# Attention through packed queries, then a squared-ReLU layer pair: two loads of the second layer's weights one place earlier, any PSUM bank for two stages, and a new order of the work

## The chip, the cores and the metric

The kernel runs on one core of one Trainium2 chip. The metric is device time in microseconds (us) of one execution; the kernel before takes 233.85 us (median of 3 runs, 233.79 to 234.32). TensorE (PE) multiplies matrices, VectorE (DVE) and ScalarE (ACT) work element by element, GpSimd (POOL) here issues nearly all loads, and SyncE (SP) issues the stores and some transposing transfers. Products of TensorE land in PSUM, eight banks of 512 float32 values in each of 128 partitions.

## The reference

```
def sm_attn(qq, kk, vv):
    s = scale * np.matmul(qq, kk.transpose(0, 1, 3, 2))
    s = s - np.max(s, axis=-1, keepdims=True)
    a = np.exp(s)
    a = a / (np.sum(a, axis=-1, keepdims=True) + 1e-09)
    return np.matmul(a, vv)
p_packed = sm_attn(p, k, v)
out = sm_attn(q, p_packed, p_packed)
...
x = out.transpose(0, 2, 1, 3).reshape(B * S, H * D)
h = x @ w_in
r = np.maximum(h, 0.0)
return (r * r) @ w_out
```

There are 8 batches of 8 heads, 576 tokens, 64 columns a head, and 32 packed queries p a head. So x has 4608 rows of 512 columns; w_in is 512 x 2048 and w_out 2048 x 512. All inputs and the output are float32; the kernel computes in bfloat16 with float32 sums.

## The kernel before

The kernel works batch by batch, and the stages of several batches overlap. For a batch b it does this, in pieces that the code names by letters, the batch, and a part:

- Tk, Tq: k and q are transposed into kT and qT (L703, L700), on VectorE for batches 0 to 4 and by transposing transfers of SP for 5 to 7.
- S1: scores of the packed queries (L736), MX their maximum (L755), EX their exponential on ScalarE (L763), E its transposes on TensorE (L769), EC the copy of these to SBUF (L611 on VectorE, L609 on ScalarE), PV the product with v (L783).
- XN, XQ, XM, XC: the packed result is divided by its sum (L792), and transposed in two ways (L796, and L802 with the copy L611).
- M: the packed result times w_in, four pieces of 512 columns (L813), and MC, their casts to bfloat16. The first layer is thus applied to the 32 packed rows of each head, and the tokens follow by the second softmax.
- S2: scores of q against the packed result (L830); SI, SM, SU transpose them and take off the maximum (L851, L857, L861), SE is the exponential on ScalarE (L864), SS the sum and its reciprocal (L867, L868), SN the division (L874), SO the transpose back into a2 (L878). For batch 0 this goes in three parts of 128, 192 and 256 tokens (SO.0.0, SO.0.1, SO.0.2), for batch 1 in two of 256 and 320 (SO.1.0, SO.1.1).
- F (batches 0 and 1, L915) or F1 (the others, L887): the first layer's output, a2 with M; R the ReLU (L923 on ScalarE, L925 on VectorE, and L897), Q or SQ the square (L933 on ScalarE, L935 on VectorE, and L905, L907) into gT. F.0.1.2 is block 2 of part 1 of batch 0.
- F2: the second layer for 128 tokens, 16 matmuls that add up over w_out's 16 blocks (L941). F2.3.1 is block 1 of token tile 3. FC copies the sum out and ST stores it (L953). For most token tiles of batches 2 to 7 a scheme with seven products of halves takes its place (GS and WS, sums of gT and w_out on VectorE, L986; GP the products, L1008; GC the adding up, L1028).

Before a wait of TensorE that the plan foresees, `keep_clock` (L615) issues matmuls on zeros, called fills here, to hold TensorE's clock.

The order is not written by hand. Each piece is an entry with its engines, its needs, and the PSUM banks or buffers it takes; `Plan.forward` goes through time as its own durations have it, and of the pieces that could start takes the one of the lowest level plus a value from `TABLE`. The order that comes out is the order of the instructions on each engine. Some groups keep the order in which they were added: all loads are one line, set by the string `ORDER`, where k0 stands for the two loads of batch 0's k, v and q alike, x and y for batch 0's q in two parts, a0 to a3 for w_in (4 pieces each), b0 to b7 for w_out, two of its 16 blocks each. A load is issued when the load eight places before it has landed (`issued[-8]`). A matmul F2 of block fb needs `LWO.(fb // 2)`, the load b(fb // 2).

E and PV take one bank each from `ONES[:3]` (banks 4, 5, 6) for batches 0 and 1, and from `ONES` (4 to 7) later; F2's tiles of batch 0 take theirs from `ONES` too. S1, S2, M and F take pairs of the banks 0 to 5 (`PAIRS`). A bank comes free when the last piece that reads it has ended, such as MC for M.

Of the kernel before, what the change touches and what calls it, by code (L numbers as in the profile page):

```python
# [14 lines left out]
P = 128  # L15
# [26 lines left out]
class Plan:  # L42
# [177 lines left out]
ORDER = ("k0 v0 x0 a0 y0 a1 a2 a3 k1 b0 b1 v1 b2 q1 b3 b4 b5 b6 b7 "  # L220
# [7 lines left out]
TABLE = {'o': {'Lk.0.0i': -36.900503, 'Lk.0.1i': 0.41924, 'Lk.0.0': -16.56608, 'LP.0': 169.009326, 'Lk.0.1':  # L228
# [292 lines left out]
def kernel_impl(tc, q, k, v, p, w_in, w_out, out):  # L521
# [23 lines left out]
    with ExitStack() as ctx:  # L545
# [485 lines left out]
        add = plan.add  # L1031
        PAIRS = [(0, 1), (2, 3), (4, 5)]
        ONES = [(4,), (5,), (6,), (7,)]
        OUTS = [(6,), (7,)]
        RS = [(8 + i,) for i in range(NR)]
        OS = [(14 + i,) for i in range(NO)][::-1]
        OP = [(14 + i, 15 + i) for i in range(0, NO - 1, 2)]
# [362 lines left out]
```

## Time and profile before

| | |
|---|---|
| median of 3 runs | 233.85 us (233.79 to 234.32) |
| the profiled execution | 233.42 us, of which the span from the first to the last instruction is 231.7 us |
| PE busy in the span | 220.0 us, 95%; 13.9 us of these are fills |
| DVE busy | 199.4 us, 86% |
| ACT busy | 148.4 us, 64% |
| POOL busy | 60.5 us, 26% |
| granted clock of TensorE | 0.994 |
| read and written in HBM | 37.22 and 9.44 MB |

In rows of a timeline the first number is the start, the second the time from the first start to the last end of the merged instructions, then engine, line, operation, tiles and shapes, and the count; in brackets stands how long the engine was idle before, and what ended it. Instructions of one engine overlap a little at their ends, so the distance from one start to the next is shorter than a length.

### The profile page before, as it was taken

To read this page: it belongs to the slowest core of one execution; us is meant where nothing else is said; L and a number is where in the kernel's file an instruction comes from. 1 tells how busy PE (TensorE), PEld (TensorE's weight loads), DVE (VectorE), ACT (ScalarE), POOL (GpSimd) and SP (SyncE) were. 2 spreads that over 40 slices of the span, in tenths; PEclk is the share of its full clock that TensorE was granted. 3 is DMA by queue.
4 is the path that set the end of the run, shared out by engine and by line. 5 is a ranking of instruction groups with operands and counts; after the bars stand their busy time and mean duration, and the time that the engine had idled before them with its cause. 6 is when DMAs were issued, how large, how long until landed. Compare 5 with 4: busy or idle time off the path is not lost.

```text
span 231.7 us, 6374 instructions
## 1 busy us (share of the span) xinstructions
PE 220.0 (95%) x2613; PEld 160.0 (69%) x2630; DVE 199.4 (86%) x336; ACT 148.4 (64%) x243; POOL 60.5 (26%) x108
## 2 busy tenths in 40 slices
PE   8978899999999999999999999999999999999991
PEld 5655664456654476768777877787668888888880
DVE  3679978999989999999999899999999997958340
ACT  3324994268955899775997936859988988310100
POOL 9787646333243575640000000000000000000010
PEclk9999999999999999999999999999999999999997
DMA  7999999999999999999999659757041001515325
GB/s 235 188 161 180 184 204 205 203 193 251 241 229 223 223 219 195 158 148 126 177 193 166 135 94 207 149 83 172 0 96 43 4 0 35 113 36 114 70 52 174
DMA packets 46668, 34.06 MB, mean 147 GB/s; under 512 B 25376, under 2 KB 38368, under 8 KB 46640
## 3 DMA queue, kind: packets, MB, share of 16 engines
q0 software_dynamic: 19488, 18.09, 50.5%
q1 hardware_dynamic: 26304, 14.98, 31.4%
q10 hardware_dynamic: 848, 0.59, 0.9%
q8 instruction: 20, 0.33, 0.6%
q14 instruction: 8, 0.07, 0.1%
HBM read 37.22 MB, written 9.44 MB: 201 GB/s over the span
## 4 chain that ended last, share of the span: by engine, by line
PE 83%; DVE 6%; DMA 5%; POOL 1%; issue 1%; ACT 1%; DVEq 0%; ACTq 0%; POOLq 0%
PE ps L1008 32%; PE ps L887 21%; PE ps L941 15%; PE ps L915 4%; PE ps L813 3%; DMA v_b<-in_v_dram 3%; DMA kq_b<-in_q_dram 2%; PE ps L959 2%; DVE gT L935 1%; PE ps L783 1%; PE ps L830 1%; PE ps L736 1%; PE ps L769 1%; POOL v_b L624 1%; DVE qT L700 1%
## 5 line engine op out<-in xcount | busy, mean ns | idle before, releaser
L897 ACT ACTIVATE r_b<-ps 128x576 bf16<-128x576 f32 x86 | 50.4, 663 | 10.1 <-PE ps L887 9.7
L887 PE MATMUL ps<-a,M 128*128 128x288 bf16 x384 | 52.3, 286 | 0.2 <-issue 0.2
L887 PEld LDWEIGHTS <-M 128*128 128x128 bf16 x384 | 37.3, 98 | 11.1 <-issue 0.2
L941 PE MATMUL ps<-w_out_b,gT 128*128 128x512 bf16 x159 | 41.3, 380 | 1.1 <-issue 0.6
L1008 PEld LDWEIGHTS <-gT 128*128 128x128 bf16 x384 | 36.9, 98 | 7.3 <-issue 1.3
L609 ACT CAST M<-ps 128x1024 bf16<-128x1024 f32 (+1 forms) x30 | 26.9, 933 | 12.4 <-PE ps L813 12.3
L609 ACT COPY o_sb<-ps 128x512 f32<-128x512 f32 (+1 forms) x23 | 12.9, 568 | 32.2 <-PE ps L1008 18.4
L1008 PEld LDWEIGHTS <-gS 128*128 128x128 bf16 x288 | 27.8, 98 | 4.5 <-issue 0.7
L953 POOL DMA_DIRECT2D out_dram<-o_sb x3 | 1.7, 556 | 108.8 <-ACT o_sb L609 103.6
L1028 DVE TENSOR_TENSOR o_sb<-o_sb,ps 128x512 f32<-128x512 f32 x30 | 20.3, 676 | 10.1 <-PE ps L1008 10.0
L907 DVE TENSOR_TENSOR gT<-r_b 128x1152 bf16<-128x1152 bf16 x37 | 27.1, 746 | 1.6 <-ACT r_b L897 1.6
L941 PEld LDWEIGHTS <-gT 128*128 128x128 bf16 x176 | 16.2, 98 | 15.4 <-issue 2.1
L1008 PE MATMUL ps<-wS,gT 128*128 128x256 bf16 x192 | 24.0, 273 | 0.0
L1008 PE MATMUL ps<-w_out_b,gT 128*128 128x256 bf16 x192 | 23.5, 273 | 0.0
L1008 PE MATMUL ps<-wS,gS 128*128 128x256 bf16 x192 | 23.3, 273 | 0.0
L923 ACT ACTIVATE r_b<-ps 128x512 bf16<-128x512 f32 (+2 forms) x30 | 17.8, 659 | 4.8 <-PE ps L915 4.7
L915 PE MATMUL ps<-a,M 128*128 128x256 bf16 (+3 forms) x160 | 18.3, 262 | 2.2 <-DVE a L878 1.0
L915 PEld LDWEIGHTS <-M 128*128 128x128 bf16 x160 | 14.0, 97 | 6.8 <-issue 2.2
L763 ACT ACTIVATE e<-ps,n 128x576 bf16<-128x576 f32 x16 | 11.7, 737 | 7.8 <-DVE n L755 7.6
L615 PE MATMUL ps<-o_sb 128*128 128x256 bf16 x89 | 13.9, 319 | 1.1 <-DVE o_sb L618 1.1
L755 DVE TENSOR_REDUCE n<-ps 128x1 f32<-128x576 f32 x16 | 11.6, 748 | 3.1 <-PE ps L736 3.0
L864 ACT ACTIVATE e<-s 128x1152 bf16<-128x1152 f32 (+4 forms) x11 | 10.0, 912 | 6.2 <-DVE s L861 6.1
(77 smaller groups left out, 322.0 us busy)
## 6 DMA issues: line engine op xcount, KB each, us to landing
out_dram<-o_sb SPq DMA_DIRECT2D x65, 128.0 KB, 3.5
kq_b<-in_k_dram POOLq DMA_DIRECT2D x14, 288.0 KB, 11.1
kq_b<-in_q_dram POOLq DMA_DIRECT2D x10, 288.0 KB, 8.7
w_in_b<-in_moe_w_in_dram POOLq DMA_DIRECT2D x16, 128.0 KB, 5.7
w_out_b<-in_moe_w_out_dram POOLq DMA_DIRECT2D x8, 256.0 KB, 9.6
v_b<-in_v_dram POOLq DMA_DIRECT2D x5, 320.0 KB, 11.8
v_b<-in_v_dram POOLq DMA_DIRECT2D x12, 128.0 KB, 8.7
v_b<-in_v_dram POOLq DMA_DIRECT2D x5, 256.0 KB, 12.2
```

Source lines behind the costliest of these rows:

```text
L609: nc.scalar.copy(dst, src)
L615: nc.tensor.matmul(half(7)[:, :2 * P], lhsT=zero[:, :P], rhs=zero, start=True, stop=True)
L755: nc.vector.tensor_reduce(n1[b % 2][:, qd:qd + 1], ps1[b, qd], axis=AX.XY if b in XBAR else AX.X, op=ALU.max, negate=True)
L763: nc.scalar.activation(e_out(qd) if b in XBAR else e1[:, qd, :S], ps1[b, qd], ACT.Exp, bias=n1[b % 2][:, qd:qd + 1], accum_out=d1[b % 2][: ...
L887: nc.tensor.matmul(t[:, c], lhsT=M[b % 2][:, qd, fb * FB:(fb + 1) * FB], rhs=a2[b % 2][:, qd, c * HALF:(c + 1) * HALF], start=(qd == 0), s ...
L897: nc.scalar.activation(dst, src, ACT.Relu)
L907: eng.tensor_tensor(out=dst, in0=r, in1=r, op=ALU.mult)
L915: nc.tensor.matmul(t[:, c, m * w:(m + 1) * w], lhsT=M[b % 2][:, qd, fb * FB:(fb + 1) * FB], rhs=a2[b % 2][:, qd, o:o + w], start=(qd == 0) ...
L923: nc.scalar.activation(dst, ph["h", b, x, j], ACT.Relu)
L941: nc.tensor.matmul(po[t], lhsT=gT[:, fb, n0:n0 + P], rhs=w_out_b[:, fb, :], start=(fb == 0), stop=(fb == NFB - 1))
L1008: nc.tensor.matmul(pz[g, k][:, i], lhsT=a[:, f, i * P:(i + 1) * P], rhs=w[:, f], start=(k not in ON and h == 0 and f == 0 and i == 0), sto ...
L1028: nc.vector.tensor_tensor(out=oC(g, i, j), in0=oC(g, *src), in1=pz[g, z], op=ALU.add)
```

## The change

Two places move in the order of loads: b0 goes ahead of batch 1's k, and b3 ahead of batch 1's q. In the built program GpSimd's queue therefore issues w_out's first piece before k1's two loads, and its fourth before q1's three. All other loads keep their order.

E and PV of batches 0 and 1 may take any of the eight banks. In the built program batch 0's still stand in bank 4; batch 1's two E are in banks 0 and 1 and its PV in bank 0, where they were in 4, 5 and 5.

`TABLE` has new values throughout, so all engines have a new order. In the first 51 us the programs differ as follows: VectorE does SS.0.0 and SI.0.2 between SI.0.1 and SO.0.0, takes the casts MC.0.0.0 and MC.0.1.1 and the ReLU R.0.1.1 and three more, and leaves the cast MC.0.2.0, one ReLU, five of batch 0's twelve squares, EC.0.0, EC.1.0 and the two casts of M.1 that it had to ScalarE, while two squares come to it from there. TensorE has F.0.1.3, F.0.0.3 and six matmuls of F2 ahead of S1.1, where one of F2 stood, and F.0.2.5, F.0.2.6 behind it. There are 97 fills for 89. Every piece before F.1.0.0 in one program stands before it in the other. On SP the stores of 11 tiles stand ahead of batch 5's key transposes for 9.

```
-ORDER = ("k0 v0 x0 a0 y0 a1 a2 a3 k1 b0 b1 v1 b2 q1 b3 b4 b5 b6 b7 "
+ORDER = ("k0 v0 x0 a0 y0 a1 a2 a3 b0 k1 b1 v1 b2 b3 q1 b4 b5 b6 b7 "
           "k2 v2 q2 k3 v3 q3 k4 v4 q4 k5 v5 q5 k6 v6 q6 k7 v7 q7")
...
-TABLE = {'o': {'Lk.0.0i': -36.900503, 'Lk.0.1i': 0.41924, 'Lk.0.0': -16.56608, 'LP.0': 169.009326, 'Lk.0.1':
...
         ONES = [(4,), (5,), (6,), (7,)]
         OUTS = [(6,), (7,)]
+        ANY = ONES + [(i,) for i in range(4)]
...
                 add(f"E.{b}.{qd}", [("PE", 0.28, lambda u, b=b, qd=qd: s1_tr(b, qd, u))], [f"EX.{b}.{qd}"] + (["I"] if b == 0 else []),
-                    line="E", take=[ONES[:3] if b < 2 else ONES], level=L + 1)
+                    line="E", take=[ANY if b < 2 else ONES], level=L + 1)
...
-                line="PV", take=[ONES[:3] if b < 2 else ONES], mode=2, level=L + 1)
+                line="PV", take=[ANY if b < 2 else ONES], mode=2, level=L + 1)
```

More of the change, by code (lines that the diff above doesn't have):

```diff
@@ L226 @@
 XTURN = (5, 6, 7)
-TABLE = {'o': {'Lk.0.0i': -36.900503, 'Lk.0.1i': 0.41924, 'Lk.0.0': -16.56608, 'LP.0': 169.009326, 'Lk.0.1':
[290 rows of a table removed]
+TABLE = {'o': {'Lk.0.0i': -55.383072, 'Lk.0.1i': 25.361911, 'Lk.0.0': 69.070364, 'LP.0': 5.218882, 'Lk.0.1':
[291 rows of a table added]
 def kernel_impl(tc, q, k, v, p, w_in, w_out, out):
```

581 rows, old and new, of the table TABLE are left out of this document.

## The prediction

> **What bounds the kernel now.** I read the table of stretches first, then the chain that ended last, then the timelines of VectorE, TensorE, ScalarE and the GpSimd queue up to 64 us. Stretches: core, us, then busy time and count of PE, PEld, DVE, ACT and POOL, granted clock, DMA share, GB/s.
>
> ```profile
> 20.00:32.00 12.00, 10.16 (x136) 7.43 (x128) 11.40 (x27) 11.21 (x21) 7.91 (x14) 1.00 1.17 184
> 32.00:51.00 19.00, 18.48 (x222) 9.51 (x207) 16.29 (x32) 9.28 (x17) 8.60 (x14) 1.00 1.22 201
> 51.00:64.00 13.00, 12.80 (x99) 8.26 (x106) 12.53 (x27) 11.88 (x22) 4.32 (x8) 1.00 1.19 242
> 64.00:100.00 36.00, 35.22 (x563) 22.03 (x554) 34.84 (x57) 27.62 (x48) 20.53 (x38) 1.00 1.20 211
> 100.00:227.00 127.00, 126.42 (x1418) 101.05 (x1406) 112.03 (x164) 82.62 (x129) 3.24 (x6) 1.00 0.58 100
> ```
>
> The reader is to see that TensorE is the bound from 32 us on: from 64 to 227 us it is idle for 36 - 35.22 + 127 - 126.42 = 1.36 us. Its work is the same in both programs. So a new order can win or lose only what TensorE waits, or spends on matmuls that merely hold the clock (fills). Most of that lies before 32 us; from 20 to 32 us TensorE is idle 1.84 us, and VectorE is busy 11.40 of 12 us. One row gives the fills; the built programs have 89 before and 97 after.
>
> ```profile
> L615 PE MATMUL ps<-o_sb 128*128 128x256 bf16 x89 | 13.9, 319 | 1.1 <-DVE o_sb L618 1.1
> 17.68 1.27 PE L615 MATMUL ps<-o_sb 128*128 128x256 bf16 x10
> ```
>
> By the first row one lasts 0.32 on the mean, the slow ones at the very start among them; by the second ten take 1.27 us with the drain of the last, some 0.11 us each.
>
> **The change, step by step.** From the start to the first block of batch 1's first layer (F.1.0.0, 50.57 us) both programs do the same pieces, fills apart. The step is therefore to find F.1.0.0's new start; then the stretch to S1.2 (63.55 us); then the rest.
>
> *Batch 0's second softmax, on VectorE.* After q has landed (row 16.48) it is one unbroken chain.
>
> ```profile
> 16.48 0.65 DVE L700 STREAM_TRANSPOSE qT<-kq_b 128x448 f32<-128x448 f32 x1 [0.35 <-DMA kq_b<-in_q_dram]
> 17.05 0.38 DVE L867 TENSOR_REDUCE t<-e 128x8 f32<-128x256 bf16 x1
> 17.58 0.58 DVE L851 STREAM_TRANSPOSE s<-ps 128x384 f32<-128x384 f32 x1
> 18.91 0.30 DVE L878 STREAM_TRANSPOSE a<-n 128x128 f32<-128x128 f32 x1
> 19.14 0.67 DVE L851 STREAM_TRANSPOSE s<-ps 128x512 f32<-128x512 f32 x1
> 19.73 0.52 DVE L861 TENSOR_TENSOR s<-s,m 128x384 f32<-128x384 f32 x1
> 23.10 0.38 DVE L878 STREAM_TRANSPOSE a<-n 128x192 f32<-128x192 f32 x1
> 24.25 0.63 DVE L611 CAST M<-ps 128x512 bf16<-128x512 f32 x1
> 25.48 0.56 DVE L935 TENSOR_TENSOR gT<-r_b 128x768 bf16<-128x768 bf16 x1
> 26.25 0.45 DVE L878 STREAM_TRANSPOSE a<-n 128x256 f32<-128x256 f32 x1 [0.22 <-PE ps L915]
> 30.48 0.65 DVE L925 TENSOR_SCALAR r_b<-ps 128x512 bf16<-128x512 f32 x1
> ```
>
> I cost an instruction by the distance to the next start. SI.0.1 (17.58) can't start earlier, since it needs the scores of the q that landed last. In the new order SS.0.0 (17.05 to 17.58, 0.53) and SI.0.2 (19.14 to 19.73, 0.59) stand between SI.0.1 and SO.0.0, which were before SI.0.1 and after SO.0.0: SO.0.0 goes from 18.91 to 20.03. The cast MC.0.0.0 that comes to VectorE (0.55, row 24.25) and SM.0.0, SU.0.0 fit into its wait for q and cost nothing; so does EC.0.0, which ScalarE now does between its two exponentials: what is late from it ends in the same wait. SO.0.1: 4.19 before after SO.0.0, now without SI.0.2 and with MC.0.1.1 (0.55): 4.15, so 24.18 for 23.10. SO.0.2: 3.15 before, without the wait (0.22), the cast (0.55) and a square (25.48 to 26.03, 0.55), with R.0.1.1, a relu of 768 columns on VectorE. That form isn't in the trace: between 0.58 (row 30.48, 512 columns, to the next start) and 1.0 (the same by 768/512 and its length of 0.65); I take 0.85, as time grows with columns. It must await F.0.1.1, itself 1.1 late, so SO.0.2 comes at 27.0 for 26.25, +0.75. The eleven extra fills ahead of F.0.1.0 (97 against 86) lie in this wait, 11 x 0.11 = 1.2; they are no second charge.
>
> *TensorE up to S1.1.* Here the earlier w_out load pays.
>
> ```profile
> 26.89 1.08 PE L915 MATMUL ps<-a,M 128*128 128x256 bf16 x8 [0.29 <-ACT r_b L923]
> 28.26 1.91 PE L915 MATMUL ps<-a,M 128*128 128x256 bf16 x16 [0.28 <-DVE M L611]
> 30.69 0.60 PE L915 MATMUL ps<-a,M 128*128 128x256 bf16 x4 [0.19 <-ACT r_b L923]
> 31.43 0.70 PE L736 MATMUL ps<-kT,pT 32*32 32x512 bf16 x32
> 42.79 7.95 PE L941 MATMUL ps<-w_out_b,gT 128*128 128x512 bf16 x35
> ```
>
> F.0.2.0 moves from 26.89 to about 27.6. Then the waits of 0.28 and 0.19 and three fills (0.33) go, as six second-layer matmuls and F.0.1.3, F.0.0.3 stand there: 0.8 back. A second-layer matmul takes 7.95 / 35 = 0.22. S1.1 has 1.3 us more work ahead of it (six of those, 1.3, and 16 first-layer matmuls, 1.1, less F.0.2.5, F.0.2.6 and one second-layer matmul, 1.1): 31.43 + 0.75 - 0.8 + 1.3, about 32.7. This is order, not loss: TensorE stands level with the old program there.
>
> *The loads.* W_out piece 0 goes ahead of k1's two, piece 3 ahead of q1's three. GpSimd's queue, and the median times to landing of just these:
>
> ```profile
> 20.81 1.19 POOL L657 DMA_DIRECT2D kq_b<-in_k_dram  x2
> 22.09 1.41 POOL L694 DMA_DIRECT2D w_out_b<-in_moe_w_out_dram  x2
> kq_b<-in_k_dram POOLq DMA_DIRECT2D x2, 288.0 KB, 6.9
> w_out_b<-in_moe_w_out_dram POOLq DMA_DIRECT2D x2, 256.0 KB, 8.4
> kq_b<-in_q_dram POOLq DMA_DIRECT2D x2, 144.0 KB, 9.9
> q0 software_dynamic: 9774, 9.52, 98.3%
> ```
>
> The k1 pair lands around 28.0, the w_out pair around 30.8: 1.4 us a piece. So k1's second half comes at about 30.1 instead of 28.8, ahead of the transpose that VectorE reaches past 31 us; q1's last third comes at about 39.9 instead of 38.5. The issues cost GpSimd nothing new, since the queue (98.3% busy up to 60 us) is the limit. The Trainium skill says otherwise of such queues: on its page SBUF — State Buffer, in the box on the "DVE blocks DMA" trap, descriptors written by GpSimd starve while VectorE holds the port pair they share. By the rows above no starving is seen, the trace doesn't bear the rule out; by it the sum would be that of the last rival below.
>
> *Batch 1.*
>
> ```profile
> 37.81 0.22 PE L802 MATMUL ps<-ident,pp 128*128 128x128 bf16 x1
> 38.61 0.63 PE L813 MATMUL ps<-w_in_b,ppT 64*32 64x512 bf16 x16
> 39.09 1.01 ACT L609 CAST M<-ps 128x1024 bf16<-128x1024 f32 x1 [2.46 <-PE ps L813]
> 40.45 0.77 DVE L700 STREAM_TRANSPOSE qT<-kq_b 128x576 f32<-128x576 f32 x1
> 42.11 0.74 PE L830 MATMUL ps<-qT,pq 32*32 32x256 bf16 x32
> 42.68 1.45 DVE L851 STREAM_TRANSPOSE s<-ps 128x512 f32<-128x512 f32 x2 [0.35 <-PE ps L830]
> 49.96 0.44 DVE L878 STREAM_TRANSPOSE a<-n 128x256 f32<-128x256 f32 x1
> 50.57 2.43 PE L915 MATMUL ps<-a,M 128*128 128x256 bf16 x20
> ```
>
> The banks: batch 1's transposes and values move from 4 and 5 to 0 and 1, which S1.1 and the exponentials have given back by then; 4 and 5 open the last two of four second-layer tiles earlier. No instruction is added, cost nothing. From S1.1 to XM.1 it was 37.81 - 31.43 = 6.4 us: now 39.1. Seven second-layer matmuls (1.5) come before M.1.0: 40.7. Both of its first casts are now on ScalarE in a row; before, one was on each engine. S2.1.0 takes the banks of M.1.0, so it waits for MC.1.0: 0.48 after M.1.0 (38.61 to 39.09) and 1.01 long, 42.2, and with VectorE's transpose of q (40.5 + 0.77 = 41.3) past: S2.1.0 at 42.5 for 42.11, +0.4. The second scores wait for the second cast, 0.9 later, but VectorE puts SM.1.0 (0.56) there. From SI.1.0 to SO.1.0 it was 7.28 us without a gap; the new order has three side jobs there (two weight sums and k2's transpose) for three sums: +0.1, taken as nothing. SO.1.0 50.4, ends 50.8, F.1.0.0 at 50.95 for 50.57. **+0.4.** Before, VectorE was ready just ahead of TensorE there (50.40); now it is late, that is the wait that replaces the old ones.
>
> *To S1.2 and on.* F.1.1.0 now stands ahead of nine second-layer matmuls and awaits SO.1.1; I take +0.05, between 0 and the 0.2 us of idle that 51 to 64 us has. On SP's queue two more tiles' stores stand ahead of batch 5's two key transposes.
>
> ```profile
> 223.89 3.71 SPq L953 DMA_DIRECT2D out_dram<-o_sb  x4
> ```
>
> Four more issues of at most 0.93 us delay these transposes by up to 3.7 us; TensorE's rows of 64 to 100 us cover them, as it works on other batches there, and if that cover is gone they cost what the idle below allows. After 64 us nothing is taken, between -1.36 (all idle gone) and +0.8 (the 0.78 of 64 to 100 us doubled).
>
> Sum: +0.45 on the profiled 233.42 us, of which the span is 231.7. That run is 0.43 below the median of 233.85, so 233.87 + 0.43 = **234.3 us**.
>
> **The rivals.** *Faster:* VectorE's lateness is eaten up and the old waits stay gone. The matmul rows show what TensorE could still win up to 43 us, 0.29 + 0.28 + 0.19 + 0.33; against it F.1.0.0 has to keep 50.57. Then the +0.4 is 0, and the new order past 64 us takes out the 0.78 idle there: 233.85 - 0.8, 233.0. It needs SO.1.0 before 50.1. For it: four open second-layer tiles give more cover. Against: the 7.28 us of VectorE have no slack.
>
> *Slower:* q1 comes too late.
>
> ```profile
> kq_b<-in_q_dram POOLq DMA_DIRECT2D x1, 288.0 KB, 11.3
> 30.29 0.72 POOL L694 DMA_DIRECT2D w_out_b<-in_moe_w_out_dram  x1 [0.72 <-DMA w_out_b<-in_moe_w_out_dram]
> ```
>
> Its last third is now issued where the second row stands, at 30.29. With the 9.9 us of these pieces it lands at 40.2, with the 11.3 of q1's first piece at 41.6. S2.1.0 at 42.5 needs it by 41.6 (transpose 0.77 and the hop). Each us past that is one on SO.1.0 and on the end: 0.8 of it, a landing at 42.4, gives 235.1; it passes 0.3% from 41.9 on. For it: the queue is full and has no slack. Against: the bytes ahead of q1 grow by one piece of 1.4 us alone.
>
> *Slower, later:* the order past 64 us doubles the 0.78 idle: 235.1.
>
> *Better through the load queue:* if VectorE's squares held up GpSimd's writing of descriptors (the mechanism of the page named above), then nine of batch 0's squares on VectorE for twelve free three times 0.37 (0.55 for 768 columns in row 25.48, by 512/768), 1.1 us, and w_out comes so much earlier: 1.1 off the forecast at most, 233.2. The 98.3% speak against it.
>
> **How the numbers follow.** This measurement tells about 0.3%, 0.7 us, from no change. The forecast (its own range 233.4 to 234.5) 0.41; q1 late 0.28; order past 64 us worse 0.11; the first, faster rival 0.18; the load queue 0.02, which ends within 0.3%. So faster 0.18, same 0.43, slower 0.39. Leaving one in ten on each side, the range is 232.9 to 235.6.
>
> **What would show it.** VectorE's L878 of 128x128 at 20.0 and of 128x192 near 24.2; the first L941 near 28 instead of 31.1; S1.1 (L736, 32 matmuls) near 32.7; L830 of 256 columns near 42.5 and waiting on ScalarE's M; L878 of 128x256 near 50.4, L915 behind it with a wait on "DVE a". If L878 comes before 50.1, the forecast fails towards faster; if a wait on in_q_dram stands before L700 near 40 us, towards slower; if F.1.0.0 is right and the end isn't, the error lies past 64 us.

## The result, and the profile after

The changed kernel takes **235.63 us** (median of 12 runs, 234.71 to 237.24), the kernel before 233.81 (12 runs, 232.60 to 234.58). The ratio is 1.007, its 95% interval 1.0045 to 1.0095: slower, by some 1.8 us. The profiled execution took 235.53 us, its span 233.7.

Two rows cut every trace into the same three legs. L852 (L851 in the kernel before) on 128x384 opens the chain on VectorE when batch 0's last part of q has landed; the first L916 (L915) on 256 columns behind 49 us is F.1.0.0, the first block of batch 1's first layer; the second group of L960 (L959) is the last product. Between the marks TensorE does the same work in both programs, fills apart; of the other engines a few weight sums, copies, stores and the transpose Tk.2.0 stand on the other side of F.1.0.0. VectorE of the kernel after, its timeline:

```profile
17.98 0.58 DVE L852 STREAM_TRANSPOSE s<-ps 128x384 f32<-128x384 f32 x1
...
20.44 0.30 DVE L879 STREAM_TRANSPOSE a<-n 128x128 f32<-128x128 f32 x1
...
24.42 0.37 DVE L879 STREAM_TRANSPOSE a<-n 128x192 f32<-128x192 f32 x1
...
27.49 0.45 DVE L879 STREAM_TRANSPOSE a<-n 128x256 f32<-128x256 f32 x1
...
39.92 1.43 DVE L701 STREAM_TRANSPOSE qT<-kq_b 128x576 f32<-128x576 f32 x2
43.28 0.72 DVE L852 STREAM_TRANSPOSE s<-ps 128x512 f32<-128x512 f32 x1 [1.94 <-PE ps L831]
...
50.83 0.40 DVE L879 STREAM_TRANSPOSE a<-n 128x256 f32<-128x256 f32 x1
```

And TensorE of the kernel after:

```profile
28.44 0.38 PE L942 MATMUL ps<-w_out_b,gT 128*128 128x512 bf16 x1
...
33.15 0.70 PE L737 MATMUL ps<-kT,pT 32*32 32x512 bf16 x32 [0.33 <-DVE r_b L926]
...
39.52 0.22 PE L803 MATMUL ps<-ident,pp 128*128 128x128 bf16 x1
...
41.18 0.63 PE L814 MATMUL ps<-w_in_b,ppT 64*32 64x512 bf16 x16
...
42.72 0.42 PE L831 MATMUL ps<-qT,pq 32*32 32x256 bf16 x16
43.08 0.82 PE L942 MATMUL ps<-w_out_b,gT 128*128 128x512 bf16 x2
43.83 0.47 PE L831 MATMUL ps<-qT,pq 32*32 32x320 bf16 x16
44.23 0.41 PE L814 MATMUL ps<-w_in_b,ppT 64*32 64x512 bf16 x8
44.57 4.71 PE L942 MATMUL ps<-w_out_b,gT 128*128 128x512 bf16 x21
49.21 0.41 PE L814 MATMUL ps<-w_in_b,ppT 64*32 64x512 bf16 x8
...
51.29 1.48 PE L916 MATMUL ps<-a,M 128*128 128x256 bf16 x12
```

The last products, kernel before and kernel after:

```profile
224.72 1.91 PE L959 MATMUL ps<-w_out_b,gT 128*128 128x256 bf16 x16
```

```profile
226.96 1.91 PE L960 MATMUL ps<-w_out_b,gT 128*128 128x256 bf16 x16
```

So the first leg took 50.57 - 17.58 = 32.99 us before and 51.29 - 17.98 = 33.31 after; the second 174.15 and 175.67. Of the 2.24 us by which the last product is later in these two executions, 0.40 is q, which landed later, 0.32 the rest of the opening, **1.52 lies past F.1.0.0**. The landing of q scatters whatever the opening: over all traces of this study the mark stands between 17.24 and 18.41 with the old opening and between 17.48 and 18.36 with the new one. The stretches of the kernel after do not show the 1.52 as idle time:

```profile
64.00:100.00 36.00, 35.10 (x549) 21.05 (x562) 33.14 (x55) 30.85 (x52) 15.74 (x29) 1.00 1.15 206
100.00:227.00 127.00, 126.34 (x1420) 100.41 (x1424) 111.02 (x164) 87.58 (x130) 6.37 (x12) 1.00 0.54 97
```

TensorE is idle 1.56 us there, for 1.36 before. Most of the time went where the profile calls TensorE busy.

Nor is this idle time all idle. A trace can lack records of matmuls: the one of the kernel before has 2613 of 2630, the one of the kernel after 2622 of 2638. A kernel of the next section has TensorE's order of before and no record missing ("before, new loads"); its second leg is the same to 0.01, and no idle time is left:

```profile
64.00:100.00 36.00, 36.00 (x555) 21.92 (x553) 34.84 (x57) 27.69 (x48) 19.92 (x36) 1.00 1.20 210
100.00:227.00 127.00, 127.00 (x1432) 101.27 (x1431) 112.83 (x166) 83.05 (x129) 3.73 (x8) 1.00 0.57 99
```

With the order of the kernel after and no record missing ("after, old loads") 0.32 us are idle there.

### The profile page after: what moved, and what is told of

The parts are those of the page before. It is cut to its first block, busy times and chain, and to the rows that moved or that the text cites. A ratio compares the mean times of both kernels' runs of the same rounds, so it can differ in the third digit from the quotient of the medians.

```text
span 233.7 us, 6390 instructions
## 1 busy us (share of the span) xinstructions
PE 220.7 (94%) x2622; PEld 159.0 (68%) x2638; DVE 195.0 (83%) x327; ACT 159.9 (68%) x252; POOL 59.5 (25%) x107
## 4 chain that ended last, share of the span: by engine, by line
PE 78%; DMA 7%; DVE 6%; ACT 4%; issue 1%; POOL 1%; SPq 1%; DVEq 0%; POOLq 0%
PE ps L1009 28%; PE ps L888 18%; PE ps L942 16%; PE ps L916 6%; PE ps L814 3%; DMA v_b<-in_v_dram 3%; DMA kq_b<-in_q_dram 2%; DMA out_dram<-o_sb 2%; ACT M L610 2%; PE ps L960 2%; PE ps L831 1%; PE ps L784 1%; PE ps L737 1%; PE ps L770 1%; DVE gT L908 1%
## 5 line engine op out<-in xcount | busy, mean ns | idle before, releaser
L898 ACT ACTIVATE r_b<-ps 128x576 bf16<-128x576 f32 x83 | 48.0, 664 | 7.4 <-PE ps L888 7.1
L942 PE MATMUL ps<-w_out_b,gT 128*128 128x512 bf16 x160 | 41.8, 379 | 1.4 <-issue 1.1
L610 ACT CAST M<-ps 128x1024 bf16<-128x1024 f32 (+1 forms) x33 | 29.9, 957 | 10.6 <-PE ps L814 9.5
L610 ACT COPY o_sb<-ps 128x512 f32<-128x512 f32 (+1 forms) x20 | 11.3, 578 | 27.2 <-PE ps L1009 13.9
L954 POOL DMA_DIRECT2D out_dram<-o_sb x2 | 1.1, 568 | 110.5 <-DVE o_sb L1029 109.3
L908 DVE TENSOR_TENSOR gT<-r_b 128x1152 bf16<-128x1152 bf16 x29 | 21.6, 748 | 3.0 <-ACT r_b L898 2.7
L1009 PE MATMUL ps<-wS,gT 128*128 128x256 bf16 x192 | 23.5, 273 | 0.4 <-DVE o_sb L1029 0.4
L906 ACT ACTIVATE gT<-r_b 128x1152 bf16<-128x1152 bf16 x19 | 22.0, 1184 | 0.4 <-DVE r_b L900 0.3
L916 PE MATMUL ps<-a,M 128*128 128x256 bf16 (+3 forms) x160 | 18.6, 262 | 0.9 <-ACT M L610 0.5
L916 PEld LDWEIGHTS <-M 128*128 128x128 bf16 x160 | 13.7, 98 | 6.1 <-DVE a L879 1.1
L924 ACT ACTIVATE r_b<-ps 128x512 bf16<-128x512 f32 (+2 forms) x25 | 15.2, 646 | 2.4 <-PE ps L803 1.3
L616 PE MATMUL ps<-o_sb 128*128 128x256 bf16 x97 | 13.3, 292 | 1.1 <-DVE o_sb L619 1.1
```

What stands on the lines that cost most here:

```text
L610: nc.scalar.copy(dst, src)
L616: nc.tensor.matmul(half(7)[:, :2 * P], lhsT=zero[:, :P], rhs=zero, start=True, stop=True)
L898: nc.scalar.activation(dst, src, ACT.Relu)
L906: nc.scalar.activation(dst, r, ACT.Square)
L908: eng.tensor_tensor(out=dst, in0=r, in1=r, op=ALU.mult)
L916: nc.tensor.matmul(t[:, c, m * w:(m + 1) * w], lhsT=M[b % 2][:, qd, fb * FB:(fb + 1) * FB], rhs=a2[b % 2][:, qd, o:o + w], start=(qd == 0) ...
```

## The experiments

In the kernels below the order that the planner gave is written out as a list of pieces with their engines, banks and fills, and `Plan.run` issues that list; a diff shows what is moved in it. Each ratio is to the kernel before as it ran beside that kernel, with medians of 233.61 to 233.90, so that ratios compare better than times. The two legs of each kernel are from its profiled execution:

| kernel | us, ratio to before (95%) | q to F.1.0.0 | F.1.0.0 to the last product |
|---|---|---|---|
| before | 233.81 | 32.99 | 174.15 |
| after | 235.63, 1.0070 (1.0045 to 1.0095) | 33.31 | 175.67 |
| before, new loads | 233.97, 1.0008 (0.9989 to 1.0027) | 32.99 | 174.16 |
| after, old loads | 237.46, 1.0158 (1.0129 to 1.0186) | 36.65 | 175.50 |
| new opening, old rest | 238.00, 1.0200 (1.0158 to 1.0241) | 33.42 | 178.48 |
| old opening, new rest | 239.86, 1.0271 (1.0242 to 1.0300) | 34.98 | 178.21 |
| before, eight more groups | 236.05, 1.0095 (1.0071 to 1.0119) | 32.99 | 176.65 |
| before, groups moved whole | 233.90, 1.0008 (0.9993 to 1.0022) | 33.00 | 174.34 |
| before, two fewer groups | 233.69, 0.9985 (0.9966 to 1.0004) | 32.95 | 174.16 |
| after, store on ScalarE's queue | 234.92, 1.0048 (1.0029 to 1.0068) | 33.32 | 175.11 |
| after, eleven fewer fills | 235.19, 1.0064 (1.0052 to 1.0076) | 33.30 | 175.11 |
| after, four fewer groups | 236.55, 1.0118 (1.0089 to 1.0147) | 33.30 | 177.21 |
| after, store and two groups | 235.15, 1.0062 (1.0038 to 1.0086) | 33.69 | 175.13 |

### The loads alone

```diff
 # the kernel after, order of loads alone
-a3 b0 k1 b1 v1 b2 b3 q1 b4
+a3 k1 b0 b1 v1 b2 q1 b3 b4
```

> The kernel after with nothing but the old order of loads: w_out piece 0 behind k1's two loads, piece 3 behind q1's three. Theory: the order of the work was made for the earlier w_out, its first second-layer matmul stands at 28.4 on TensorE and w_out lands at about 30.8 with the old loads, so TensorE stops there for 2.4 us and S1.1 comes at 35 or later; half of it at least stays to the end: 1 to 2.4 us over the kernel after, 236.6 to 238. Rival (the load order does harm in itself, k1 and q1 come late): 0.3 to 0.7 under the kernel after, 235.0 to 235.3.

And the reverse edit in the kernel before:

> The kernel before with nothing but the new order of loads. In the old order of work k1's second half is transposed at 29.79 and q1's last third at 40.45. Theory: w_out's earlier piece serves nobody there, k1's second half lands 1.4 us later, near 30.1, so its transpose comes 0.3 to 0.5 late and q1 with 39.9 is still in time: 0 to 0.5 over the kernel before, 233.8 to 234.3. Rival of the prediction (q1 too late): a wait on in_q_dram ahead of L700 near 40 us, and 0.8 over, 234.6 or more.

The old loads in the new order give 237.46 us. TensorE of that kernel:

```profile
30.09 0.38 PE L942 MATMUL ps<-w_out_b,gT 128*128 128x512 bf16 x1 [1.99 <-DMA w_out_b<-in_moe_w_out_dram]
```

The second-layer matmul that stands at 28.44 in the kernel after waits 1.99 us for w_out, and S1.1 comes at 35.99. The new loads in the old order change nothing that can be told: 233.97, the legs are those of before. K1's two halves are transposed on VectorE as soon as before, counted from q. The second half in the kernel before, then both with the new loads:

```profile
29.79 0.77 DVE L703 STREAM_TRANSPOSE kT<-kq_b 128x576 f32<-128x576 f32 x1
```

```profile
29.30 0.78 DVE L704 STREAM_TRANSPOSE kT<-kq_b 128x576 f32<-128x576 f32 x1
...
30.67 0.78 DVE L704 STREAM_TRANSPOSE kT<-kq_b 128x576 f32<-128x576 f32 x1
```

That trace has q at 18.41; 30.67 is 12.26 behind it, and 29.79 was 12.21 behind 17.58 in the kernel before. So the load order does no harm and no good by itself: the rival of a late k1 or q1 falls, and the new order of work needs the new loads.

### One half of each order

```diff
 # pieces up to F.1.0.0 in the order of one kernel, the rest in that of the other
-all pieces of one planner's order
+pieces[:F.1.0.0] of the one, then what is left in the order of the other; banks handed out anew
```

> The new program's order up to the first block of batch 1's first layer (F.1.0.0), the old program's order behind it; same work. The after trace loses 0.8 us to F.1.0.0 and 2.0 at the end. Theory A (the loss is a sum of places: about 0.8 in the opening, about 1.2 past 64 us from the new order there): 0.8 over the kernel before, 234.4 to 234.8, F.1.0.0 near 51.3. Rival B (the late opening causes all, the rest only answers to it): 1.6 to 2.0 over, 235.4 to 235.8. Rival C (the rest alone loses, the opening's delay is eaten up): 233.8.

> The reverse: the old order with the old load order and banks up to F.1.0.0, the new order behind it. Theory A: 1.0 to 1.2 over the kernel before, 234.8 to 235.0, F.1.0.0 at 50.5, the waits near 183 us (TensorE on ScalarE's r_b) and 218 us (TensorE on the stores out of o_sb) still there. Rival B: 233.8, these waits gone. Rival C: 235.4 to 235.8.

None of the three theories holds: both are slower than either kernel, so the joint itself costs. With the new opening TensorE waits behind F.1.0.0 for VectorE's squares of batch 0 and 1, which the old rest has in another place:

```profile
54.36 0.39 PE L942 MATMUL ps<-w_out_b,gT 128*128 128x512 bf16 x1 [0.96 <-DVE gT L936]
```

This is the longest of several such waits, and explains a part only of the 4.3 us by which that second leg is longer than the kernel before's. In the other kernel TensorE has the order of before up to F.1.0.0, and the banks handed out anew already cost 2 us there. As a test of where the loss lies the pair is inconclusive; of use is that the new opening again takes 33.4.

### The groups of small tiles

TensorE works in arrays of 128*128, and for some pieces in smaller ones: 32*32 for S1 and S2, 64*32 for M, 128*32 for PV (the shape stands behind the names in each row). I call a stretch of such pieces between full ones a group. From F.1.0.0 on the old order has 23 groups, the new 27; from S1.1 to F.1.0.0 five and six. The kernel before shows the price on pieces of one shape:

```profile
94.18 1.04 PE L1008 MATMUL ps<-wS,gS 128*128 128x256 bf16 x8
95.15 0.84 PE L813 MATMUL ps<-w_in_b,ppT 64*32 64x512 bf16 x24
95.92 1.05 PE L1008 MATMUL ps<-wS,gS 128*128 128x256 bf16 x8
96.80 1.91 PE L1008 MATMUL ps<-w_out_b,gT 128*128 128x256 bf16 x16
98.55 1.04 PE L1008 MATMUL ps<-wS,gT 128*128 128x256 bf16 x8
```

Eight full matmuls take 0.875 (96.80 to 98.55 are sixteen). From 94.18 to 95.92 are eight full ones and three M pieces: 1.74, so three pieces cost 0.87. The eight more groups come by pulling pieces apart:

```diff
 # TensorE's order in the kernel before, one of the places
-GP.0.2.1 GP.1.2.0 M.3.1 M.3.2 M.3.3 GP.1.2.1 GP.2.2.0 GP.2.2.1 GP.3.2.0 M.4.0 M.4.1 M.4.2 GP.3.2.1
+GP.0.2.1 M.3.1 GP.1.2.0 M.3.2 GP.1.2.1 M.3.3 GP.2.2.0 M.4.0 GP.2.2.1 M.4.1 GP.3.2.0 M.4.2 GP.3.2.1
```

> The kernel before, in which eight pieces on TensorE (M.2.1, M.3.1, M.3.3, M.4.0, M.4.1, S2.4.1, PV.6, M.7.0) stand one to three blocks of full-array matmuls away from the small-tile matmuls beside which they stood; loads, VectorE, ScalarE and GpSimd in the old order. In the traces a lone M piece (16 matmuls of 64x32 tiles) takes 0.44 us out of a row of full matmuls, two 0.65, three 0.87: 0.22 a piece and 0.22 more for each stretch of such tiles, a group. The new order has 27 groups past F.1.0.0 where the old has 23, and one more ahead of it. Theory G (each group costs its 0.22 at the end): 8 x 0.22 = 1.8 over the kernel before, 235.4 (235.0 to 235.8). Rival (only waits count, the change lost its time to waits): the pieces are ready earlier than they are used, so no wait comes, 233.5 to 233.9.

The control also moves eight pieces, five of them the same, but whole groups:

```diff
 # TensorE's order in the kernel before, one of the places
-GP.0.2.1 GP.1.2.0 M.3.1 M.3.2 M.3.3 GP.1.2.1
+GP.0.2.1 M.3.1 M.3.2 M.3.3 GP.1.2.0 GP.1.2.1
```

> Control to the run with eight more groups. The kernel before, in which eight pieces on TensorE (M.2.1, M.2.2, M.3.1, M.3.2, M.3.3, M.4.0, M.4.1, M.4.2) are also moved, one block of full matmuls ahead, but each group as a whole, so that the number of groups stays 23. Theory G: no change, 233.6 to 234.1. Rival (moving these pieces costs by itself, for example through their casts or banks): 234.5 to 236, as with the eight more groups.

With eight more groups 236.05 us, with groups moved whole 233.90. The kernel with eight more:

```profile
94.70 0.41 PE L814 MATMUL ps<-w_in_b,ppT 64*32 64x512 bf16 x8
95.05 1.05 PE L1009 MATMUL ps<-wS,gS 128*128 128x256 bf16 x8
96.02 0.41 PE L814 MATMUL ps<-w_in_b,ppT 64*32 64x512 bf16 x8
...
143.04 0.55 PE L784 MATMUL ps<-v_b,e 128*32 128x64 bf16 x40 [0.64 <-DMA e<-e]
```

One piece and eight full matmuls take 96.02 - 94.70 = 1.32, so a piece by itself costs 0.44 where a piece among three costs 0.29, with no idle time in these rows. The second leg grew by 2.50 us; 0.64 is a wait that the moved PV.6 met, the rest 1.86, or **0.23 a group**. Theory G holds for these eight; the wait was not foreseen. The Trainium skill has the mechanism on its page TensorEngine Tiling (Array Packing), section Key Properties: a change of the tiling mode, not of the tile alone, drains TensorE. It gives no figure; here a change of shape costs about half of 0.23 (an estimate, as a group has a change into it and one out of it).

It does not follow that the new order loses 4 x 0.23 past F.1.0.0. Four PV pieces that stood beside S1 or M before stand alone in it, and between PV and its neighbour the shape changed anyway. PV.2 behind S1.3 adds 0.43 (the two take 1.16, S1.2 alone 0.73, in the kernel before with new loads), by itself it takes 0.52. Added up over all rows of groups, in the two traces in which no matmul record is missing, it is 17.46 us for 23 groups (before with new loads) and 17.82 for 27 (after with old loads): **+0.36**. It is nearly all in the way into a group: from a group's first small matmul to the full one behind it, both add up to 15.3. Ahead of F.1.0.0 the sums are 3.34 and 3.64 (S1.1 without its wait): +0.30. S2.1.0, S2.1.1 with M.1.2, and M.1.3 stand there in three groups (42.72, 43.83, 49.21) where two stood.

### Fewer groups

```diff
 # the kernel after, TensorE, ScalarE and VectorE
-S2.1.0 F2.0.8 F2.0.9 S2.1.1 M.1.2 ... F2.2.10 ... F2.1.15 M.1.3
+S2.1.0 S2.1.1 F2.0.8 F2.0.9 ... F2.2.10 M.1.2 M.1.3 ... F2.1.15
-MC.1.1 on ScalarE, MC.1.2 ahead of SE.1.0
+MC.1.1 on VectorE, MC.1.2 and MC.1.3 behind SE.1.0
-M.2.1 F2.6.9 F2.6.10 M.2.2; S2.3.1 F2.5.14 ... M.3.0; S1.6 GP.4.3.1 ... PV.5
+F2.6.9 F2.6.10 M.2.1 M.2.2; S2.3.1 M.3.0 F2.5.14 ...; PV.5 S1.6 GP.4.3.1 ...
```

> The kernel after with four groups fewer: S2.1.1 right behind S2.1.0 (for that MC.1.1 is cast on VectorE, idle there from 41.3 to 43.3), M.1.3 behind M.1.2 and both casts behind SE.1.0; M.2.1 beside M.2.2, M.3.0 beside S2.3.1, PV.5 beside S1.6. Theory G: 4 x 0.22 = 0.9 under the kernel after (1.007 of the kernel before), so 234.5 to 234.9; SI.1.1 (L852) comes 0.5 earlier. Rival (waits, not groups): 235.3 to 235.8, as no wait that the after trace shows past 64 us is touched.

A clear miss: 236.55 us, slower than the kernel after. The groups went, waits came. S2.1.1 had to wait for the cast that went to VectorE (it ends at 43.55, S2.1.1 follows), and at 137.87 PV.5 stands still:

```profile
137.87 0.53 PE L784 MATMUL ps<-v_b,e 128*32 128x64 bf16 x40 [0.76 <-DMA e<-e]
```

The wait for a landing store, told in the next section, is 0.72 long there, for 0.39 in the kernel after. SI.1.1 did not come earlier either, since VectorE takes it behind SM.1.0. The second try leaves M.2.1 and PV.5 where they were and adds the store of the next section:

> The kernel after with what the last runs left standing: tile 30 stored from ScalarE's queue, and two groups fewer (S2.1.1 beside S2.1.0 and M.1.3 beside M.1.2, with MC.1.1 on VectorE; M.3.0 beside S2.3.1). M.2.1 and PV.5 stay where the new order has them, since moving them brought waits of 0.2 for E.3.0, 0.8 for PV.5 and 0.2 for XM.5 in the run with four fewer. Theory G: 0.5 for the store and 2 x 0.22 for the groups under the kernel after: 1.003 of the kernel before, 234.5 to 234.8 beside 233.8. Rival (the gain of a group is always given back in a wait): 234.9 to 235.3, as with the store alone.

It gave 235.15, no better than the store alone (234.92). Two rows of its TensorE tell why:

```profile
36.93 0.38 PE L942 MATMUL ps<-w_out_b,gT 128*128 128x512 bf16 x1 [0.22 <-DMA w_out_b<-in_moe_w_out_dram]
...
97.00 0.41 PE L814 MATMUL ps<-w_in_b,ppT 64*32 64x512 bf16 x8 [0.16 <-ACT M L610]
```

With M.3.0 moved up, M.3.3 waits for the cast that frees its bank. And in this execution q had landed at 17.49, early, and TensorE then waited for w_out: the new order has its second-layer matmuls close behind the loads, so that the early q didn't help it here. In the kernel before the same was tried in two places:

```diff
 # TensorE's order in the kernel before
-S2.2.1 F2.8.8 ... M.2.0; S2.3.0 F2.5.13 S2.3.1
+S2.2.1 M.2.0 F2.8.8 ...; F2.5.13 S2.3.0 S2.3.1
```

> The kernel before with two groups fewer: S2.3.0 beside S2.3.1, M.2.0 right behind S2.2.1; nothing else. Theory G: 2 x 0.22 = 0.45 under the kernel before, 233.2 to 233.4, the best kernel so far. Rival (the groups' time lies under something else): 233.6 to 233.8.

The median is 0.2 lower and its interval holds no change; the second leg is the same to 0.01. From F1.2.0 (82.28 before, 82.07 here) to S2.4.0 (103.02, 102.58) it is 0.23 shorter, the gain of S2.3.0; between S1.2 and F1.2.0, where M.2.0 was moved, 0.17 were lost. There the ten transposes E of batch 3 take 0.84 to the next matmul (72.72 to 73.56), for 0.57 before (73.19 to 73.76): that matmul starts just behind ScalarE's copy of a finished tile, which ends at 73.50, so a wait took back what M.2.0 may have saved. That a group less is a gain at the end is not shown by any run; that a group more is a loss is.

### The store

The chain of the kernel after (start, length, engine and line), around two waits that the kernel before does not have:

```profile
181.98 0.66 ACT r_b L898
182.76 0.66 ACT r_b L898
183.46 0.65 PE ps L888 x4
...
210.89 0.70 DVE o_sb L1029
211.61 0.53 SPq L954
212.19 0.60 SPq L954
212.83 0.60 SPq L954
213.47 3.90 DMA out_dram<-o_sb
217.49 0.70 DVE o_sb L1029
218.23 1.03 PE ps L1009 x8
```

At 183.46 TensorE waits for ScalarE's ReLU; that costs 0.26, by the distance to the matmul before. At 218.23 it waits for VectorE, and VectorE for o_sb, whose old content is still being stored.

```diff
-add(f"ST.{t}", [("SP", 1.25, lambda t=t: store(t))], done, ...)
+add(f"ST.{t}", [("SP", 1.25, lambda t=t: store(t, eng=nc.scalar if t == 30 else nc.sync))], done, ...)
```

> The kernel after, where token tile 30 is stored from ScalarE's queue instead of behind tile 29 on SP's. In the after trace TensorE waits at 218.2 us for VectorE's o_sb, which waits for the four stores issued on SP from 211.6 to 214.1, the last landing at 217.4. With two queues the last is issued 1.2 earlier and lands near 216.2, when VectorE's input is there. Theory: the wait of 0.55 before and at GP.3.7.0 goes and the end comes 0.4 to 0.6 earlier, 235.0 to 235.3 for 235.6. Rival (something as late stands behind it, or ScalarE's issues hold up its casts): no change, 235.5 to 235.8.

It takes 234.92; the second leg is 0.56 shorter. ScalarE's queue, VectorE and TensorE of that kernel:

```profile
211.65 1.46 ACTq L954 DMA_DIRECT2D out_dram<-o_sb  x2
```

```profile
216.78 0.68 DVE L1029 TENSOR_TENSOR o_sb<-o_sb,ps 128x512 f32<-128x512 f32 x1
```

```profile
217.72 1.04 PE L1009 MATMUL ps<-wS,gT 128*128 128x256 bf16 x8
```

The wait is gone, and nothing as late stands behind it. But it also goes by itself: the next kernel has its stores as the kernel after, all on SP's queue, and in its profiled execution VectorE passes there without a wait, with a second leg as short, 175.11:

```profile
216.89 0.68 DVE L1029 TENSOR_TENSOR o_sb<-o_sb,ps 128x512 f32<-128x512 f32 x1
```

Of four traces with the kernel after's order of stores three have the wait on TensorE (0.39, and 0.21 and 0.72 in "after, old loads" and "after, four fewer groups"), and neither of the two with the store moved. "New opening, old rest" has it too, 0.73, so it isn't bound to the new order. The intervals of the two ratios, with the store moved and without, overlap. That the other queue takes the wait away is likely, and not shown by the times.

### The fills

```diff
 # the kernel after, ahead of M.0.1
-keep_clock(20)
+keep_clock(9)
```

> The kernel after with 9 fills instead of 20 ahead of M.0.1 at 20.4 us. The prediction charged the eleven extra fills nothing, since they lie in the wait for SO.0.0. Theory: TensorE idles 1.2 us more there and M.0.1 starts where it did, 235.5 to 235.9, as the kernel after; the granted clock stays at 1.00 from 20 to 32 us. Rival (the fills hold up M.0.1 and F.0.0.0): 0.2 to 0.5 faster, 235.1 to 235.4. Other rival (the clock falls without them): the granted clock below 1.00 and 0.3 or more slower.

235.19 us, a ratio of 1.0064 beside the 1.007 of the kernel after: no difference that can be told. The stretch of this kernel:

```profile
20.00:32.00 12.00, 9.61 (x111) 7.36 (x110) 11.82 (x29) 10.11 (x18) 8.28 (x13) 1.00 1.17 184
```

TensorE is busy 9.61 us from 20 to 32 us, for 10.73 in the kernel after; the granted clock stays at 1.00, and the first leg is 33.30 as with the fills.

## Why the prediction was right or wrong

The time, 235.63, lies at the very edge of the range (232.9 to 235.6); the likeliest case, no change, was wrong, and slower (0.39) came. **Up to F.1.0.0 the sum was right.** With the 0.40 us that q came later taken off, the marks are, forecast and measured: SO.0.0 20.03 and 20.04, SO.0.1 24.18 and 24.02, SO.0.2 27.0 and 27.09, the first second-layer matmul 28 and 28.04, S1.1 32.7 and 32.75, XM.1 39.1 and 39.12, M.1.0 40.7 and 40.78, S2.1.0 42.5 and 42.32, SO.1.0 50.4 and 50.43, F.1.0.0 50.95 and 50.89. Part of this is luck. S1.1 is in time with a wait of 0.33 for VectorE's ReLU (the row at 33.15) that the sum doesn't have, so the work ahead of it had been put some 0.3 too high. S2.1.0 came 0.18 earlier than forecast, and from SI.1.0 to SO.1.0 VectorE took 7.55 us for 7.28, where the sum took nothing: the two make up for each other. The charge of nothing for the fills and for the loads held in runs of their own.

**The reason given at F.1.0.0 was right, though the wait that was to show it is missing.** VectorE was to be late there and TensorE to wait for it. VectorE's transpose ends at 51.23, as forecast if q's delay is taken off, and F.1.0.0 starts 0.06 later. In the kernel before a block of the first layer that does wait for such a transpose, the one at 18.91 that ends at 19.21, starts 0.06 behind it too:

```profile
19.27 0.61 PE L915 MATMUL ps<-a,M 128*128 128x128 bf16 x8 [0.32 <-DVE a L878]
```

The row of F.1.0.0 has no idle time because TensorE, with one group more to do, got there at the same moment. A group less does not help while VectorE is no earlier. "After, four fewer groups" has one less ahead of F.1.0.0, and the same distance:

```profile
51.20 0.41 DVE L879 STREAM_TRANSPOSE a<-n 128x256 f32<-128x256 f32 x1
```

```profile
51.66 2.90 PE L916 MATMUL ps<-a,M 128*128 128x256 bf16 x24
```

Its first leg is 33.30, as in the kernel after. The prediction said of the bank change that it costs nothing. No run has the new order with E and PV in their old banks, so this stays open. The torn groups of M.1 and S2.1 do not come of it: in the kernel before, too, four second-layer tiles are open in banks 4 to 7 when M.1.2, M.1.3 and S2.1 run, and these use the same two pairs of banks in two groups. It is the new order that puts S2.1.0 between them. That other banks can cost much is shown by "old opening, new rest", 2 us in the first leg.

**The step that failed is "after 64 us nothing is taken", with its bounds of -1.36 to +0.8.** The last check named in the prediction tells it: F.1.0.0 right and the end not. The stretch to S1.2 held: it took 13.28 us for 12.98, with one second-layer matmul (0.22) more ahead of S1.2. Measured past F.1.0.0 is +1.52 in the profiled pair, and +0.96 where the store doesn't wait. Of these 0.96, 0.36 are groups, 0.26 the wait for ReLU, and about 0.3 lie in many steps under 0.15 that were not told apart. The store's wait adds the other 0.56. The bounds had been made from idle time alone: the steps into a group count as busy, and the 1.36 us that a better order was to win, the 0.78 that a worse one was to double, were no idle time, as the trace without missing records shows. And a new wait at the very end, behind a landing store, was not looked for, though the stores on SP were listed.

Of the rivals, q1's late landing fell (its transposes, from 39.92 on, have no wait on the load). So did the load queue, whose 233.2 is far from 235.63; in the new order TensorE even waited for w_out in an execution where q was early (the row at 36.93). The slower rival past 64 us had the right place and nearly the right size, 235.1, but gave the doubling of an idle time that wasn't there as the reason.

## What to carry to other kernels

Where one engine is busy all the time, compare two orders by the time between marks that do the same work, and not by idle time: a change of array shape cost about 0.11 us here that the profile books as busy, and missing records of matmuls look like idle time. Count the changes of shape in an order before pricing it, and look at who needs the banks and the casts before tearing groups apart or joining them, since a joined group that waits for one of them can give back more than it saves. And look at the last 20 us by themselves: a buffer that waited for a store to land had nothing behind it there to hide the wait.

## What the runs showed of the hardware

A group torn off cost 0.23 us beside its pieces. About 0.09 of it is the way into tiles of 64*32 (in the kernel before the eight full matmuls from 94.18 would end at 95.06, and M starts at 95.15); the rest, by difference, is the way out. Batch 0's q, with the same loads ahead of it in every program, was ready at times that differed by 1.2 us from one execution to another (17.24 to 18.41), and took the whole opening with it. Four stores issued one behind the other on SP's queue took 3.90 us from the last issue to the landing; with half of them on ScalarE's queue VectorE started on that buffer without a wait, 0.71 earlier, as it also did once with all four on SP's.
